# Gate scaling and two kinds of copies moved from VectorE to ScalarE in a fused transform, routing and expert kernel

## The chip, the cores and the metric

The kernel runs on one core of a Trainium2 chip. The metric is the device time of one execution in microseconds (us), lower is better. Engines are called as in the profile: PE is TensorE, DVE is VectorE, ACT is ScalarE, POOL is GpSimd, SP is SyncE, which only issues transfers. Each engine works through its own queue in order; a queue whose first instruction waits holds everything behind it.

## The reference

Three stages follow one another.

1. A spectral layer on x (4 x 3072 x 256): a real Fourier transform over the 3072 positions, a complex 256x256 product with bias, a soft threshold of 0.01, and the inverse transform. The result is read as 12288 rows of 256 numbers.
2. A routed expert layer with 8 experts and room for 384 rows in each. A row goes to the expert with its largest logit (row times a 256x8 matrix), if a place is left in order of the rows, and the output is scaled by the softmax weight of that expert, the gate:

```python
h = np.maximum(np.einsum('ecd,edf->ecf', disp, w1), 0.0)
y = np.einsum('ecf,efd->ecd', h, w2)
out[i] = gate_w[i] * y[expert_idx[i], pos[i]]
```

3. A dense layer: `h = x @ w_in` (256 to 2048), `g = h * sigmoid(h)`, `g @ w_out` (2048 to 256). Rows without a place are zero all through.

## The kernel before, in words

All matmuls that need it are made of three products of rounded parts: a number is split into a rounded part ("hi", cast by ACT at L192) and the remainder ("lo", a subtraction by DVE or POOL at L200), and `mm3` (L206) issues hi x hi, lo x hi and hi x lo. So each tile that PE reads has an ACT cast and a DVE or POOL subtraction ahead of it.

The first part of the kernel (`near`, to about 175 us) does the spectral layer of the first batch and the forward part of the second, and routes the first 3072 rows. The kernel then turns only as many rows of the second batch as it needs to fill the experts: `third` (L569) does the inverse transform of a third of that batch in four blocks of 512 columns. In it `rows` loads the spectrum that `kphase` stored (its last blocks are copied by ACT at L495 through `hi`, L192) and turns it by matmuls; ACT copies the result to SBUF (L595) and SP stores it. `gate` (L600) transposes the rows on PE, **copies the transposed rows from PSUM (L606)**, multiplies them by the gate matrix, and for every second block chooses the expert of each row on DVE (`choose`). `route` (L696) then gives each row its place, and `slots` (L804) makes the list of rows and gate weights `gw` for each expert.

`experts` (L949) runs the experts in the order 0, 1, 2, first pair, 3, 4, second pair, 5, 6, third pair, 7, fourth pair; `third` and `route` run beside experts 0 to 2. For each expert:

- `gather` (L1078) fetches its 384 rows by three indirect transfers that POOL issues.
- `turn` (L1092) **scales each of the three 128-row pieces by the gate weight of its rows (L1095)**, one number per partition, transposes the pieces on PE (L1102), and splits the result (ACT cast, DVE remainder). The gate weight is not negative, so it can be applied ahead of the layer. For all but the first expert the turn is issued in step 6 of the part before, and `behind` ties the scaling to a DVE instruction of step 5 there; the tie is an order for the planner and no semaphore.
- `first_ffn` (L1106) makes the hidden layer in 8 steps: PE fills a PSUM tile, ACT rectifies it (L1120), DVE makes the remainder (L1121), PE multiplies with the second weights. At its end **the two halves of the expert's output are copied from PSUM: the first by ACT (L1130), the second by DVE (L1131)**.
- `weights` (L1051) loads weight pieces through four buffers by SP (L1066), ACT casts them and DVE or POOL makes the remainders.

`pair` (L1133) takes the outputs of two experts, combines them by additions and subtractions on DVE (L1151 to L1159) and splits the combinations into `ms` tiles; `second_ffn` (L1166) runs the dense layer on both with seven products in place of eight per block, the gated unit by ACT (L1199), and writes the rows out by indirect transfers.

The order within each engine's queue isn't written out by hand: the program is traced in the order of the code, and a planner that simulates the engines' times settles the order of every queue when the kernel is built (`schedule_with_timeline_sim=True`, L1387). A change of an instruction's engine can so change the order of others too.

Of the kernel before, what the change touches and what calls it, by code (L numbers as in the profile page):

```python
# [12 lines left out]
ALU = mybir.AluOpType  # L13
AF = mybir.ActivationFunctionType
# [121 lines left out]
def raw(t):  # L136
    return t.bitcast(F32)
# [18 lines left out]
class Kernel:  # L156
# [412 lines left out]
    def third(self, b, res):  # L569

        nc, bp, ps, wg, CH = self.nc, self.bp, self.ps, self.wg, self.CH
        v = nc.vector
        c4 = self.c4[:Q, 64:]
        bv = self.bds[b].rearrange("k (r u g) c -> (k r) u (g c)", r=4, u=4)
        od = self.attn[0][b * S:b * S + QB * TW].rearrange("(q u g) d -> u q (g d)", u=4, g=GT)
        res[b] = self.chosen(1)
        idle = self.mg.tile([P, 3, 2, CH], F32, tag="ms", name="bi", bufs=1)
        room = {n + 2: idle[:Q, n] for n in range(3)}
        room[5] = self.mh.tile([P, 2, CH], F32, tag="yT", name="by", bufs=1)[:Q]

        def rows(n):
            pt = ps.tile([P, CH], F32, tag="ps", name="ps2")
            for w in range(2):
                br = room.get(2 * n + w)
                if br is None:
                    br = bp.tile([Q, 2, CH], F32, tag="xt", name="br", bufs=self.sb)
                nc.sync.dma_start(out=br, in_=bv[:, 2 * w:2 * w + 2, n * CH:(n + 1) * CH])
                for z in range(2):
                    u = 2 * w + z
                    ins = nc.tensor.matmul(pt[u * QB:(u + 1) * QB], c4, br[:, z], start=True, stop=True).ins  # L590
                    if b == 1 and not u:
                        self.after(ins, self.lasty)
            ao = bp.tile([P, 2, 2, P], F32, tag="ao", name="ao2")
            aof = ao.rearrange("p g h d -> p (g h d)")
            nc.scalar.copy(aof, pt)  # L595
            for u in range(4):
                nc.sync.dma_start(out=od[u, :, n * CH:(n + 1) * CH], in_=aof[u * QB:(u + 1) * QB])
            return ao

        def gate(n, ao):  # L600
            tp = ps.tile([P, 2, 2, P], F32, tag="ps", name="tp")
            for g in range(2):
                for h in range(2):
                    nc.tensor.transpose(tp[:, g, h], ao[:, g, h], self.ident)
            aT = bp.tile([P, 2, 2, P], F32, tag="aT", name="aT", bufs=1)
            v.tensor_copy(aT, tp)  # L606
            if n % 2 == 0:
                self.lg = ps.tile([P, P], F32, tag="ps", name="lg")
            for h in range(2):
                for g in range(2):  # L610
                    at = COL * (2 * (n % 2) + g)
                    nc.tensor.matmul(self.lg[at:at + COL], wg[:, h], aT[:, g, h], start=h == 0, stop=h == 1)
            if n % 2:
                ls = bp.tile([P, P], F32, tag="ls", name="ls", bufs=1)
                nc.scalar.copy(ls, self.lg)
                lt = ps.tile([P, 4, COL], F32, tag="ps", name="lt")
                nc.tensor.transpose(lt.rearrange("p g e -> p (g e)"), ls, self.ident)
                self.choose(lt.rearrange("p (o g) e -> p o g e", o=1)[:, :, :, :E], res[b], slice(2 * n - 2, 2 * n + 2))

        ao = {}  # L620
        for n in range(GT // 2 + 1):
            if n < GT // 2:
                ao[n] = rows(n)
            if n:
                gate(n - 1, ao.pop(n - 1))
            yield

    def is2(self, b, qbs, res):
# [58 lines left out]
        for g in range(GT + 2):  # L687
            if g < GT:
                ao[g] = rows(g)
            if 0 < g <= GT:  # L690
                aT[g - 1] = turn(ao.pop(g - 1))
            if g > 1:
                gate(g - 2, aT.pop(g - 2))
            yield
# [397 lines left out]
    def turn(self, rows, behind=None):  # L1092
        xg, gw = rows
        for j in range(SC):
            ins = self.nc.vector.tensor_scalar(xg[:, j], xg[:, j], gw[:, j:j + 1], None, ALU.mult)  # L1095
            if behind:
                self.after(ins.ins, behind)
        xT = self.mx.tile([P, 2, 2, CAP], FR, tag="xT", name="xT")
        for h in range(2):
            tp = self.ph.tile([P, CAP], F32, tag="hp", name="gtp")  # L1100
            for j in range(SC):
                self.nc.tensor.transpose(tp[:, j * P:(j + 1) * P], xg[:, j, h * P:(h + 1) * P], self.ident)  # L1102
            self.split("av", xT[:, 0, h], xT[:, 1, h], tp)
        return xT

    def first_ffn(self, e, xT, ws):  # L1106
        nc, mp, pm = self.nc, self.mh, self.pm
        NJ = F // P
        w1, w2 = ws
        yp = [pm.tile([P, 2 * D], F32, tag="y", name=f"y{h}")[:, :CAP] for h in range(2)]  # L1110
        hs = {}
        for j in range(NJ + 1):
            if j < NJ:
                hp = self.ph.tile([P, CAP], F32, tag="hp", name="hp")
                for h in range(2):
                    w, c = w1[j // 2], slice(j % 2 * P, (j % 2 + 1) * P)
                    self.mm3(hp, w[:, 0, h, c], w[:, 1, h, c], xT[:, 0, h], xT[:, 1, h], h == 0, h == 1)
                hh = mp.tile([P, CAP], FR, tag="hh", name="hh")
                hl = mp.tile([P, CAP], FR, tag="hl", name="hl")
                self.rectified = nc.scalar.activation(hh, hp, AF.Relu).ins  # L1120
                self.evicted = nc.vector.scalar_tensor_tensor(hl, hp, 0.0, raw(hh), ALU.max, ALU.subtract).ins  # L1121
                hs[j] = hh, hl
            if j > 0:
                hh, hl = hs.pop(j - 1)
                for h in range(2):
                    w, c = w2[(j - 1) // 2], slice(h * P, (h + 1) * P)
                    self.lasty = self.mm3(yp[h], w[:, 0, (j - 1) % 2, c], w[:, 1, (j - 1) % 2, c], hh, hl, j == 1, j == NJ)[1]
            yield
        y = self.ys[e] = self.mg.tile([P, 2, CAP], F32, tag="yf", name="yf", bufs=3)
        nc.scalar.copy(y[:, 0], yp[0])  # L1130
        nc.vector.tensor_copy(y[:, 1], yp[1])  # L1131

    def pair(self, behind=None):  # L1133

# [256 lines left out]
```

## Time and profile before

| what | us |
|---|---|
| median of 3 runs (lowest to highest) | 616.54 (615.39 to 617.16) |
| time of the profiled execution | 617.55 |
| its span, first to last instruction | 615.8 |
| PE busy in the span | 593.4 |
| DVE busy | 424.7 |
| ACT busy | 339.3 |
| POOL busy | 187.0 |

The profile is of one execution; its times are counted from its first instruction. "L1095" is line 1095 of the kernel. A matmul row gives the shape of the weights and the moving data; a row with "xN" merges N instructions that follow one another. Rows of neighbouring instructions on one engine overlap by about 0.09 us. What stands in brackets behind a row is the time that the engine stood still before it and what ended that. PEclk is the granted clock of TensorE as a share of its upper level (2.4 GHz; the lower, 1.2 GHz, is 0.50).

### The profile page before, as it was taken

Reading aid. Unit: us, or ns where it says so; the run is one execution under the profiler, and the core shown is the slowest. Engines: PE = TensorE matmul, PEld = TensorE weight load, DVE = VectorE, ACT = ScalarE, POOL = GpSimd, SP = SyncE. Lnnn points to the kernel's source line nnn. Section 1 sums busy time; section 2 is a strip of 40 time slices with the busy share of each in tenths; the row PEclk is TensorE's granted clock in tenths of the full one; section 3 lists DMA queues with packets and bytes.
Section 4 is the critical chain, followed back from the end, with each engine's and each line's share of the span. In section 5 each row is a group of like instructions: output and inputs, shape, how many; then the busy total and the mean of one; then the engine's idle time right before and its main releaser. Section 6 shows DMA issues by size and latency. Waiting matters only on the chain. (4 is left out here: it accounts for less than half of the span.)

```text
span 615.8 us, 11426 instructions
## 1 busy us (share of the span) xinstructions
PE 593.4 (96%) x4104; PEld 556.1 (90%) x4104; DVE 424.7 (69%) x844; ACT 339.3 (55%) x723; POOL 187.0 (30%) x189
## 2 busy tenths in 40 slices
PE   9999999999989799899999999999999999999994
PEld 9887799667988589789999999999999999989994
DVE  2468765449977589998876786587587577486563
ACT  2546554336525465556765756655567556365562
POOL 1001110002053023177453505435403442154433
PEclk9999999999999799989999999999999999999998
DMA  8829775996357976433633532404433230010001
GB/s 223 254 78 277 249 219 168 250 278 180 105 183 209 248 226 191 143 120 99 197 120 116 169 125 97 155 23 138 150 113 106 91 100 26 0 65 27 16 2 56
DMA packets 65755, 86.09 MB, mean 140 GB/s; under 512 B 5812, under 2 KB 55608, under 8 KB 65688
## 3 DMA queue, kind: packets, MB, share of 16 engines
q1 hardware_dynamic: 53720, 69.53, 37.8%
q10 hardware_dynamic: 9664, 9.44, 5.2%
q0 software_dynamic: 2304, 6.29, 3.2%
q8 instruction: 34, 0.56, 0.4%
q14 instruction: 33, 0.27, 0.2%
HBM read 54.31 MB, written 30.93 MB: 138 GB/s over the span
## 5 line engine op out<-in xcount | busy, mean ns | idle before, releaser
L1289 DVE TENSOR_TENSOR u<-h,u 128x384 f32<-128x384 f32 x224 | 117.9, 552 | 59.9 <-PE h L210 51.6
L1199 ACT ACTIVATE u<-u 128x384 f32<-128x384 f32 x128 | 64.6, 522 | 73.1 <-DVE u L1289 71.1
L209 PE MATMUL o<-wo,gl 128*128 128x256 f32 x354 | 94.5, 280 | 0.9 <-DVE gl L200 0.9
L210 PE MATMUL o<-wo,gh 128*128 128x256 f32 x354 | 94.6, 280 | 0.0
L208 PE MATMUL o<-wo,gh 128*128 128x256 f32 x354 | 83.1, 280 | 0.0
L200 POOL TENSOR_TENSOR ring<-mt,ring 128x384 fp32r<-128x384 f32 x32 | 38.0, 1190 | 136.3 <-ACT ring L192 136.3
L200 POOL TENSOR_TENSOR gl<-u,gh 128x384 fp32r<-128x384 f32 x62 | 64.8, 1060 | 29.6 <-ACT gh L192 29.5
L209 PEld LDWEIGHTS o<-wo,gl 128*128 128x128 f32 x354 | 66.5, 188 | 1.2 <-DVE gl L200 1.2
L210 PEld LDWEIGHTS o<-wo,gh 128*128 128x128 f32 x354 | 66.5, 188 | 0.0
L192 ACT CAST gh<-u 128x384 fp32r<-128x384 f32 x126 | 63.1, 509 | 5.7 <-PE o L210 4.0
L208 PEld LDWEIGHTS o<-wo,gh 128*128 128x128 f32 x354 | 62.4, 188 | 0.0
L208 PE MATMUL yp<-wri,xk 128*128 128x256 f32 x188 | 56.1, 298 | 0.0
L210 PE MATMUL yp<-wri,xk 128*128 128x256 f32 x188 | 54.0, 287 | 0.0
L209 PE MATMUL yp<-wri,xk 128*128 128x256 f32 x188 | 53.7, 286 | 0.0
L192 ACT CAST w<-st 128x512 fp32r<-128x512 f32 x64 | 38.6, 619 | 23.5 <-DMA st<-in_moe_w 15.7
L200 DVE TENSOR_TENSOR w<-st,w 128x512 fp32r<-128x512 f32 x56 | 39.6, 717 | 17.1 <-ACT w L192 12.0
L1120 ACT ACTIVATE hh<-hp 128x384 fp32r<-128x384 f32 x64 | 31.1, 489 | 35.4 <-PE y L209 13.7
L1121 DVE SCALAR_TENSOR_TENSOR hl<-hp,hh 128x384 fp32r<-128x384 f32 x64 | 34.9, 552 | 21.6 <-ACT hh L1120 16.3
L200 POOL TENSOR_TENSOR wi<-na,wi 128x256 fp32r<-128x256 f32 (+1 forms) x8 | 8.1, 1012 | 132.9 <-ACT wi L192 132.9
L208 PE MATMUL hp<-xT,w 128*128 128x384 f32 x128 | 43.8, 343 | 4.2 <-ACT w L192 4.1
L200 DVE TENSOR_TENSOR gl<-u,gh 128x384 fp32r<-128x384 f32 x64 | 42.8, 669 | 2.2 <-ACT gh L192 2.1
L208 PE MATMUL y<-hh,w 128*128 128x384 f32 x128 | 43.7, 341 | 0.5 <-ACT hh L1120 0.5
(254 smaller groups left out, 1543.1 us busy)
## 6 DMA issues: line engine op xcount, KB each, us to landing
st<-in_moe_w SPq DMA_DIRECT2D x64, 256.0 KB, 2.9
out<-zt SPq DMA_DIRECT2D x48, 256.0 KB, 3.5
b_d<-bo ACTq DMA_DIRECT2D x12, 512.0 KB, 3.1
mt<-mixed SPq DMA_DIRECT2D x32, 192.0 KB, 2.3
xt<-in_x SPq DMA_DIRECT2D x15, 384.0 KB, 6.7
nt<-in_moe_w_in SPq DMA_DIRECT2D x8, 512.0 KB
nt<-in_moe_w_out SPq DMA_DIRECT2D x16, 256.0 KB, 3.0
a_d<-ao SPq DMA_DIRECT2D x8, 384.0 KB, 3.4
```

The costliest lines, as they stand in the source:

```text
L192: self.lastact = self.nc.scalar.copy(dst, src)
L200: return e.tensor_tensor(dst, src, raw(hi), ALU.subtract).ins
L208: first = nc.tensor.matmul(out, lh, rh, start=start, stop=False)
L209: nc.tensor.matmul(out, ll, rh, start=False, stop=False)
L210: return first.ins, nc.tensor.matmul(out, lh, rl, start=False, stop=stop).ins
L1120: self.rectified = nc.scalar.activation(hh, hp, AF.Relu).ins
L1121: self.evicted = nc.vector.scalar_tensor_tensor(hl, hp, 0.0, raw(hh), ALU.max, ALU.subtract).ins
L1199: act.activation(sg, sg, AF.Silu)
L1289: v.tensor_tensor(to, h, u, ALU.add)
```

## The change

Three kinds of instructions go from DVE to ACT: the scaling of the gathered rows by their gate weight (24 instructions, 128x256 each, an ACT activation with function Copy and a scale of one number per partition), the copy of the transposed rows of the turned third (4 instructions, 128x512) and the copy of the second half of the expert outputs (8 instructions, 128x384). The data, the tiles and the transfers are the same.

```diff
@@ gate, in third
-            v.tensor_copy(aT, tp)
+            nc.scalar.copy(aT, tp)
@@ turn
-            ins = self.nc.vector.tensor_scalar(xg[:, j], xg[:, j], gw[:, j:j + 1], None, ALU.mult)
+            ins = self.nc.scalar.activation(xg[:, j], xg[:, j], AF.Copy, scale=gw[:, j:j + 1])
@@ first_ffn
         nc.scalar.copy(y[:, 0], yp[0])
-        nc.vector.tensor_copy(y[:, 1], yp[1])
+        nc.scalar.copy(y[:, 1], yp[1])
```

## Rows read from the trace of the kernel before

**Rows 1.** The page's busy times of the engines, share of the span, instructions.

```profile
PE 593.4 (96%) x4104; PEld 556.1 (90%) x4104; DVE 424.7 (69%) x844; ACT 339.3 (55%) x723; POOL 187.0 (30%) x189
```

**Rows 2.** Stretches: bounds, length, busy time of each engine, PEclk, DMA share, GB/s.

```profile
178.00:186.00 8.00, 6.11 (x42) 5.37 (x41) 5.75 (x12) 3.44 (x7) 6.21 (x6) 1.00 0.79 247
...
204.60:211.30 6.70, 6.69 (x24) 4.59 (x25) 3.00 (x5) 2.87 (x6) 0.00 (x0) 0.50 1.09 258
...
262.20:266.00 3.80, 3.80 (x13) 3.70 (x13) 3.05 (x10) 0.68 (x1) 3.49 (x3) 0.55 0.24 72
...
290.00:598.00 308.00, 306.89 (x2085) 305.31 (x2084) 213.53 (x395) 187.77 (x403) 118.44 (x111) 1.00 0.29 92
```

**Rows 3.** Groups that the change removes: busy us, mean ns, idle before.

```profile
L1095 DVE TENSOR_SCALAR xg<-xg,gwt 128x256 f32<-128x256 f32 x15 | 9.7, 699 | 0.0
...
L1131 DVE COPY yf<-y 128x384 f32<-128x384 f32 x8 | 4.4, 555 | 1.4 <-PE y L210 1.2
...
L1095 DVE TENSOR_SCALAR xg<-xg,gws 128x256 f32<-128x256 f32 x9 | 3.6, 438 | 2.2 <-DMA xg<-attn,srcs 2.2
...
L606 DVE COPY aT<-tp 128x512 f32<-128x512 f32 x4 | 2.7, 675 | 0.0
```

**Rows 4.** Groups of ACT nearest to what the change adds, same columns.

```profile
L462 ACT ACTIVATE xk<-xk 128x256 fp32r<-128x256 f32 x22 | 9.1, 416 | 0.0
...
L1130 ACT COPY yf<-y 128x384 f32<-128x384 f32 x8 | 3.8, 470 | 2.0 <-PE y L210 2.0
...
L753 ACT ACTIVATE pm<-iota,r 128x128 fp32r<-128x128 f32 x8 | 2.4, 389 | 0.6 <-DVE r L737 0.6
...
L595 ACT COPY ao<-ps 128x512 f32<-128x512 f32 x4 | 2.3, 585 | 1.9 <-PE ps L590 1.9
...
L462 ACT ACTIVATE xk<-xk 128x128 fp32r<-128x128 f32 x2 | 0.6, 298 | 0.0
```

**Rows 5.** In order of time, first turn: start, us, instruction, idle before.

```profile
178.26 1.32 ACT L192 CAST w<-st 128x512 fp32r<-128x512 f32 x2 [6.47 <-DMA st<-in_moe_w]
...
179.48 0.58 ACT L192 COPY bo<-bp 128x512 f32<-128x512 f32 x1
...
179.99 0.35 DVE L1095 TENSOR_SCALAR xg<-xg,gws 128x256 f32<-128x256 f32 x1 [2.17 <-DMA xg<-attn,srcs]
...
182.67 0.34 DVE L1095 TENSOR_SCALAR xg<-xg,gws 128x256 f32<-128x256 f32 x1
...
183.07 0.44 PE L1102 MATMUL gtp<-ident,xg 128*128 128x128 f32 x2 [0.93 <-DVE xg L1095]
...
183.84 0.58 ACT L192 COPY bo<-bp 128x512 f32<-128x512 f32 x1 [3.77 <-PE gtp L1102]
...
184.47 1.13 PE L494 MATMUL bp<-cl,c 128*128 128x256 f32 x4 [0.97 <-ACT bo L192]
```

**Rows 6.** In order of time, the first pair.

```profile
260.40 0.44 PE L208 MATMUL h<-ms,wi 128*128 128x384 f32 x1 [1.22 <-ACT ms L192]
260.53 0.55 DVE L1131 COPY yf<-y 128x384 f32<-128x384 f32 x1
...
262.17 0.45 PE L210 MATMUL h<-ms,wi 128*128 128x384 f32 x1 [1.15 <-DVE ms L200]
```

**Rows 7.** ACT and PE in order of time, second turn and weights.

```profile
203.94 0.62 ACT L192 CAST w<-st 128x512 fp32r<-128x512 f32 x1 [5.88 <-DMA st<-in_moe_w]
...
204.61 0.69 PE L208 MATMUL hp<-xT,w 128*128 128x384 f32 x1 [4.11 <-ACT w L192]
...
207.74 1.54 PE L1102 MATMUL gtp<-ident,xg 128*128 128x128 f32 x6
...
207.90 0.59 ACT L595 COPY ao<-ps 128x512 f32<-128x512 f32 x1 [1.95 <-PE ps L590]
```

**Rows 8.** ACT and DVE in order of time, the last copy of the third.

```profile
237.74 0.62 ACT L192 CAST wo<-na 128x512 fp32r<-128x512 f32 x1 [2.37 <-DVE na L900]
...
238.10 0.67 DVE L606 COPY aT<-tp 128x512 f32<-128x512 f32 x1
```

## The prediction

> **What bounds the kernel now.** I read the page's line of busy times first, then a table of stretches, then the order of time around every stretch in which PE stands still. The first shows PE busy in 593.4 us of a span of 615.8, DVE in 424.7 and ACT in 339.3 [rows 1]. The change touches only DVE and ACT, so it can be worth something only where PE waits for one of them. The table of stretches says where that is: from 290 to 598 us PE is busy for 306.9 of 308.0 us, so at most 1.1 us is to be had there [rows 2]. What the change can reach lies between 178 and 266 us, in three places.
>
> - The first turn (expert 0): PE waits 0.93 us for the third scaling of gathered rows and 0.97 us for a copy of ACT [rows 5].
> - The weights of the first experts: PE waits 4.11 us for a cast of ACT that itself waited for a weight load [rows 7], and then runs 6.7 us at a mean granted clock of 0.50, the lower of its two levels (1.2 GHz), which costs 6.7 x 0.50 = 3.4 us [rows 2].
> - The first pair: PE waits 1.22 us for a cast and 1.15 us for a remainder of the combined expert outputs [rows 6], and the clock then averages 0.55 for 3.8 us, which costs 3.8 x 0.45 = 1.7 us [rows 2].
>
> **Prices.** Removed from DVE: 24 scalings, 9.7 + 3.6 us; four copies of the turned third, 2.7 us; eight copies of half an expert output, 4.4 us: 20.4 us together [rows 3]. Added to ACT: a copy of the turned third has the form of the ACT copy at L595, 0.585 us; a copy of half an output that of L1130, 0.470 us, so 4 x 0.585 + 8 x 0.470 = 6.1 us [rows 4]. A scaling by ACT whose factor is one number per partition is not in the trace. Without such an operand, 128x256 takes 0.416 us and 128x128 takes 0.298 (L462); with one, 128x128 takes 0.389 (L753). The low end is therefore 0.416; the high end is 0.389 + (0.416 - 0.298) = 0.507. I take 0.50, near the high end, because the operand is there: 24 x 0.50 = 12.0 us. ACT comes to 339.3 + 18.1 = 357.4 us and DVE to 404.3; neither becomes the bound of the whole.
>
> The Trainium skill, in "ScalarE: Activation LUTs", section "What ACT_TABLE_LOAD costs", gives 186 ns plus 0.833 ns per element and about 93 ns more for each pointer operand. By that a scaling would be an estimated 0.49 us, and the 24 of them 11.8 us instead of 12.0.
>
> **The first turn.** In the trace ACT casts two weight pieces at 178.26, copies a spectrum block at 179.48 until 180.06, and then stands still until 183.84, when PE's transposes of the gathered rows end [rows 5]. DVE begins the first scaling at 179.99, as its gather lands, and the third at 182.67, with no wait for a transfer listed [rows 5]. So the third gather had landed before 182.67, by how much is not shown. If it was there by 181.6, ACT, idle from 180.06, ends the third scaling at 182.1, against 182.67 + 0.34 = 183.01 now; if it came only at 182.67, at 183.17. I take the first, since DVE shows no wait there: PE's wait of 0.93 shrinks by 0.9 us. The wait of 0.97 us moves along, because the copy that ends it is released by the same transposes. The best case loses both waits, 1.9 us. The worst is a price of the in-order queue: if the planner sets the scalings ahead of the two casts and the copy at 178.26 to 180.06, those 1.8 us follow the last scaling, and PE's matmuls behind that copy come up to 1.7 us later. No DMA is moved; the gathers stay on POOL and the weight loads on SP.
>
> **The second and third turn, the weights.** The 4.11 us wait ends with a weight load, and the DMA share is 1.09 in the stretch after it [rows 2, 7]. Three scalings off DVE do not move that: zero. The tie of the scalings to a DVE instruction of the step before ("behind") now names another engine; it is an order for the planner and no semaphore. What could be lost here is the second rival.
>
> **The first pair.** DVE's copy of half an output stands at 260.53 in front of the remainders on which PE waits until 262.17 [rows 6]. Without it those come 0.47 us earlier (0.555 less the overlap of neighbours of some 0.09). On ACT the added copy follows the one of the first half and delays the casts behind it by about 0.4 us, so the first wait grows from 1.22 to some 1.6 us while the second ends at 261.7: a gain of 0.5 us, between 0 and the whole 2.4. The clock is the larger term. PE's waits here, 2.37 us, were followed by the lower level; the 1.90 us of the first turn were not (1.00 over 178 to 186 us) [rows 2, 5, 6]. With 1.9 us left I count half of the 1.7 us, 0.9, and keep both ends.
>
> **Five later turns and the other copies: zero.** Their cover is the full queue of PE. The scalings of these turns average 0.699 us, where the one at 182.67 took 0.34, twice as long, and PE has no more than 1.1 us of idle time in the whole stretch [rows 2, 3, 5]. If the cover were thinner on ACT, where the step's rectified outputs queue behind three scalings of 1.3 us together, a turn would lose part of that; I keep +2 us for the five as the end.
>
> **Sum.** 0.9 + 0.5 + 0.9 = 2.3 us. The profiled execution took 617.55 us (span 615.8 and 1.75 around it), 1.0 above the median of the runs, 616.54; against itself it goes to 615.25, and the median goes to 614.2.
>
> **Rivals.**
>
> *The route is relieved too (chance 0.14).* The last copy of the turned third starts at 238.10 on DVE, while ACT stands still for 2.37 us until 237.74 [rows 8]. If the planner lets ACT do it there, the logits, the choice and the route come up to 2.3 us earlier, DVE reaches the pair that much sooner, and all of 2.37 + 1.7 = 4.1 us goes. With 0.9 of the first turn: 616.54 - 5.0 = 611.5. Against it: the planner fixes PE's order, and PE may take the logits no earlier.
>
> *Nothing moves (0.27).* The third gather lands late, the casts of the pair are pushed back by the copy that was put on ACT, the clock falls as before: 616.5. For it speaks that each gain stands behind a chain of several engines.
>
> *Slower, through ACT's queue in the second turn (0.23).* DVE scaled the rows of expert 1 at 200 us, while ACT stood 5.88 us at the weight cast of 203.94 [rows 7]. On ACT the scalings can come only before that cast or after it. If they come after the copy of the third that starts at 207.90 and ends at 208.49, they end at 209.8, and PE's transposes, now at 207.74, slip by 2.1 us; the engine is then at the lower level and stays there about as much longer, which costs half of that, 1.0 more. That is +3.1, and with nothing gained elsewhere 619.6. It decides from the point where the first of these scalings starts later than 207.74 - 1.3 = 206.4. Against it: before the cast ACT is free from 198.06 to 203.94, and the rows have long landed.
>
> A rule of the Trainium skill speaks for this side: "ScalarE: Activation LUTs", "Rules for kernel authors", tells authors to use VectorE, not ScalarE, for a multiplication or an addition. The rows agree as to one instruction, 0.34 us on DVE at 182.67 [rows 5] against my 0.50; by the rule alone the change would give away time on each turn, while the mean of 0.699 on DVE in the later turns goes against it.
>
> **How the numbers follow.** My forecast has 0.36, its own range 612.5 to 615.5. About 0.3% of the time, 1.85 us, is what a measurement of this kernel can tell from no change: below 614.7 is faster, above 618.4 slower. Of the forecast 0.31 lies below 614.7 and 0.05 above; with the relieved route's 0.14, faster is 0.45. The same: 0.05 + 0.27 + 0.01 = 0.33. Slower: 0.22 of the 0.23. The range runs from the relieved route, 611.3, to just short of the worst of the slower case, 619.3.
>
> **What would show it.** Right: the third scaling ends by 182.2 on ACT and PE's wait for it is below 0.2 us; ACT's scalings take 0.49 to 0.51; PE's wait at 262 us is near 0.7 and the half-clock stretch behind it shorter or gone; the 4.1 us wait for weights stays; from 290 us on PE's idle time stays near 1.1. Wrong: another order of the weight loads on SP, which would change the 4.1 us either way; a PE wait on the gathered rows in the second or third turn; new waits of PE for rectified outputs behind the scalings of later turns.

## The result: 0.8% slower, and the profile after

The changed kernel takes 621.36 us, median of 20 runs (618.58 to 626.12), against 616.56 for the kernel before in the same session (20 runs): ratio 1.0079, 95% interval 1.0060 to 1.0097. The forecast was 614.2 with a range up to 619.3; direction and range were both wrong. The profiled execution took 624.49 us, its span is 622.7.

The page's line of busy times answers to [rows 1]:

```profile
PE 592.7 (95%) x4104; PEld 553.0 (89%) x4104; DVE 408.0 (66%) x808; ACT 353.0 (57%) x759; POOL 182.9 (29%) x189
```

DVE lost 16.7 us, ACT gained 13.7, and PE does the same 4104 matmuls in the same time; the span is 6.9 us longer. So PE stands still more. The stretches, with the columns of [rows 2], say where:

```profile
178.00:186.00 8.00, 6.51 (x41) 5.39 (x41) 5.16 (x9) 4.70 (x10) 5.58 (x5) 1.00 0.78 249
...
262.20:266.00 3.80, 3.41 (x18) 2.77 (x17) 3.66 (x10) 2.40 (x6) 1.46 (x2) 1.00 0.00 0
290.00:342.00 52.00, 52.00 (x365) 52.00 (x364) 37.07 (x65) 34.68 (x77) 21.01 (x21) 1.00 0.42 130
342.00:374.00 32.00, 27.48 (x159) 26.48 (x158) 19.35 (x36) 18.38 (x40) 9.19 (x9) 1.00 0.44 135
374.00:598.00 224.00, 223.54 (x1531) 221.79 (x1530) 140.19 (x267) 139.14 (x302) 85.98 (x81) 1.00 0.25 78
290.00:598.00 308.00, 303.02 (x2051) 300.27 (x2050) 196.61 (x367) 192.20 (x416) 116.18 (x111) 1.00 0.30 93
```

In the kernel before, the fourth of these stretches reads:

```profile
342.00:374.00 32.00, 32.00 (x193) 31.63 (x192) 27.00 (x51) 22.34 (x49) 9.67 (x10) 1.00 0.46 145
```

All idle time that PE gained after 290 us lies between 342 and 374 us, 4.5 us of it, where expert 3 ends and expert 4 begins. I call that place the crossing. In the list of PE's waits over the whole execution (who waited, for whom: us in total, times, longest us), the second line, for the copy of half an output, is the longest single wait and lies at the crossing; of the first line 1.2 us do, and the other three lie before 290 us:

```profile
PE y L210 <- DVE hl L1121: 4.0, 4, 1.9
PE y L208 <- ACT yf L1130: 3.3, 1, 3.3
PE hp L208 <- ACT w L192: 2.6, 1, 2.6
PE y L208 <- ACT hh L1120: 1.9, 2, 1.5
PE lg L612 <- ACT aT L606: 1.4, 1, 1.4
```

The groups that were added to ACT (columns as in [rows 3]):

```profile
L1095 ACT ACTIVATE xg<-xg,gwt 128x256 f32<-128x256 f32 x15 | 6.5, 499 | 0.0
...
L1095 ACT ACTIVATE xg<-xg,gws 128x256 f32<-128x256 f32 x9 | 4.1, 503 | 1.7 <-DVE cl L487 1.3 <-DMA xg<-attn,srcs 0.4
L1131 ACT COPY yf<-y 128x384 f32<-128x384 f32 x8 | 3.9, 488 | 0.0
...
L606 ACT COPY aT<-tp 128x512 f32<-128x512 f32 x4 | 2.3, 581 | 0.0
```

The prices were right: 0.499 and 0.503 us for a scaling (0.50 forecast), 0.488 and 0.581 for the copies (0.470 and 0.585). (ACT's total came to 353.0 and not to 357.4, DVE's to 408.0 and not to 404.3: the forecast added up single prices, and neighbouring rows overlap by some 0.09 us, which makes about 3 us of either difference.) The estimate by the Trainium skill ("ScalarE: Activation LUTs", "What ACT_TABLE_LOAD costs"), 0.49 for a scaling, agrees with the trace too. The time was not lost on prices.

### The profile page after: what moved, and what is told of

It is laid out like the page before. It is cut to its first block, busy times and chain, and to the rows that moved or that the text cites. A ratio compares the mean times of both kernels' runs of the same rounds, so it can differ in the third digit from the quotient of the medians.

```text
span 622.7 us, 11433 instructions
## 1 busy us (share of the span) xinstructions
PE 592.7 (95%) x4104; PEld 553.0 (89%) x4104; DVE 408.0 (66%) x808; ACT 353.0 (57%) x759; POOL 182.9 (29%) x189
## 5 line engine op out<-in xcount | busy, mean ns | idle before, releaser
L200 POOL TENSOR_TENSOR ring<-mt,ring 128x384 fp32r<-128x384 f32 x32 | 36.6, 1144 | 134.6 <-ACT ring L192 131.9
L200 POOL TENSOR_TENSOR gl<-u,gh 128x384 fp32r<-128x384 f32 x62 | 63.5, 1041 | 39.1 <-ACT gh L192 37.8
```

The costliest lines, as they stand in the source:

```text
L200: return e.tensor_tensor(dst, src, raw(hi), ALU.subtract).ins
```

## The experiments

Each was timed beside the kernel before on the same chip; the ratio is to that. "Crossing" below is also a time: from PE's first transpose of expert 4's rows to the first L1230 of the second pair, the product that opens its output rows: 24.9 us before, 30.0 after. In edits that add lines, the line numbers of the rows are up to 8 higher.

### One part at a time

In the four expectations of this group theory A blames the scalings, theory B the copies of half an output, and theory C the copies of the turned third. Behind them the letters are given anew.

**Only the scalings on ACT** (the hunk of `turn` alone):

> Only the 24 scalings go to ACT; the copy of the turned third and the half outputs stay on DVE. Theory A (the scalings, set three in a row into ACT's queue ahead of the copies of finished output rows and of the rectified step outputs, are what PE pays for): 3 to 6 us slower than before, with a new wait of PE of over 1 us where expert 3 ends. Theory B (the half-output copies, queued on ACT behind a rectified output that waits, hold the PSUM tile of the next expert): 0 to 1 us from before, no such wait. Theory C (the relief of the turned third moves the order around 240 to 255 us): within 1 us of before, with the 2.4 us of PE waits at the first pair as before.

Measured: 622.01 us, ratio 1.0101 [1.0076, 1.0126]. PE waits 2.0 us at the crossing, runs 3.4 us at the lower clock behind it, and the crossing takes 28.9 us: what A expected.

**Only the copies of half an output** (the hunk of `first_ffn` alone):

> Only the eight half-output copies go to ACT. Theory A: within 1 us of before. Theory B: 3 to 6 us slower, with PE waiting over 1 us on the copy at L1130 or L1131 where expert 3 ends. Theory C: within 1 us of before; at the first pair the second wait of PE about 0.5 us shorter.

Measured: 616.91 us, ratio 1.0011 [0.9998, 1.0024]; PE waits 0.2 us at the crossing.

**Only the copies of the turned third** (the hunk of `gate` alone):

> Only the four copies of the turned third go to ACT. Theories A and B: within 1 us of before, from 290 us on unchanged. Theory C: the wait of PE moves from the first pair (2.4 us at 260 us) to remainders of the last expert step before it (1.9 us at 251 us in the changed kernel), and the time is 1 to 2 us above before.

Measured: 614.29 us, ratio 0.9962 [0.9942, 0.9983]: faster, where theory C had expected one to two microseconds more.

**The whole change once more**, in the same session:

> The changed kernel once more, for a second trace: 621.4 us, 4.8 above before. Theory A and B: the 3.3 us wait of PE near 352 us, on the first half copy of expert 3's output, is there again, within 1 us. If it is under 1 us here, the stall of that one execution is chance and cannot carry the median's 4.8 us.

Measured: 620.18 us, ratio 1.0069 [1.0049, 1.0090]; crossing 30.5 us, and PE's wait is there again, 2.8 us long. The parts, +5.6, +0.5 and -2.1 us by medians against 616.39, add up to +4.0, the whole is +3.8. The scalings are what costs.

### What happens at the crossing

ACT's queue there, in the changed kernel:

```profile
340.75 1.31 ACT L1095 ACTIVATE xg<-xg,gwt 128x256 f32<-128x256 f32 x3
341.97 1.05 ACT L1240 COPY tail<-o 128x512 f32<-128x512 f32 x2
...
348.62 0.49 ACT L1120 ACTIVATE hh<-hp 128x384 fp32r<-128x384 f32 x1 [1.09 <-PE hp L210]
352.23 0.62 ACT L192 CAST w<-st 128x512 fp32r<-128x512 f32 x1 [3.12 <-PE hp L210]
354.38 0.49 ACT L1120 ACTIVATE hh<-hp 128x384 fp32r<-128x384 f32 x1 [1.53 <-remote]
354.77 0.47 ACT L1130 COPY yf<-y 128x384 f32<-128x384 f32 x1
```

and two of PE's instructions:

```profile
348.58 0.33 PE L210 MATMUL hp<-xT,w 128*128 128x384 f32 x1
...
355.29 0.44 PE L208 MATMUL y<-hh,w 128*128 128x384 f32 x1 [3.26 <-ACT yf L1130]
```

Read them together. The three scalings are over at 342.06; they are not in the way of anything at 350. The weight cast of 352.23 waits for the matmul that began at 348.58 and took 0.33 us, the last reader of its buffer: it starts 3.3 us after that matmul's end. The copy behind it in ACT's queue comes at 354.77, and PE waits 3.26 us for the PSUM tile that this copy empties. The weight load had landed by 345 us. So for some microseconds PE's finished work is not seen by the engines that wait for it. The trace holds the semaphore events of PE, by which it tells the others that a matmul is done; set against the ends of matmuls (which the profile models), 585 of 628 come within 0.02 us, but here they are up to 3.89 us late.

What else ran there is on POOL. Before, the indirect transfers that write the first pair's rows out (L1337, two for each third of the rows, called scatters below) and the gathers of expert 6 (L1084) are spread from 333 us:

```profile
333.15 1.02 POOL L1337 DMA_INDIRECT out<-tail,dsts  x1 [3.79 <-ACT tail L1240]
334.48 1.00 POOL L1337 DMA_INDIRECT out<-tail,dsts  x1 [0.30 <-issue]
339.52 1.34 POOL L1337 DMA_INDIRECT out<-tail,dsts  x1 [4.04 <-ACT tail L1240]
341.17 0.98 POOL L1337 DMA_INDIRECT out<-tail,dsts  x1 [0.30 <-issue]
342.46 1.44 POOL L1337 DMA_INDIRECT out<-tail,dsts  x1 [0.30 <-issue]
...
348.15 1.00 POOL L1084 DMA_INDIRECT xg<-attn,srct  x1 [0.30 <-issue]
```

After, nine of them follow one another every 1.3 us:

```profile
342.81 1.02 POOL L1337 DMA_INDIRECT out<-tail,dsts  x1 [10.39 <-ACT tail L1240]
344.14 1.00 POOL L1337 DMA_INDIRECT out<-tail,dsts  x1 [0.30 <-issue]
...
353.28 1.16 POOL L1084 DMA_INDIRECT xg<-attn,srct  x1 [0.30 <-issue]
```

What releases the scatters of a row third is ACT's copy of it (L1240). Before, the three copies came at 332.3, 338.7 and 340.6:

```profile
332.29 0.58 ACT L1240 COPY tail<-o 128x512 f32<-128x512 f32 x1 [0.33 <-PE o L210]
338.66 0.59 ACT L1240 COPY tail<-o 128x512 f32<-128x512 f32 x1 [0.34 <-PE o L210]
340.64 0.59 ACT L1240 COPY tail<-o 128x512 f32<-128x512 f32 x1 [0.68 <-issue]
```

With the scalings on ACT the planner sets the copies of the first two row thirds behind them, and all three start between 342.0 and 343.3 us. It also set PE's own order anew: the products that close the first two thirds end at 340.9 and 341.2 there, so that without the scalings these copies could have come about 1 us earlier and no more.

```profile
340.64 0.28 PE L210 MATMUL o<-wo,gh 128*128 128x256 f32 x1
...
340.88 0.40 PE L210 MATMUL o<-wo,gh 128*128 128x256 f32 x2
```

That gave theory A: the unbroken run of indirect transfers makes PE's completions late. Theory B: the scalings hold ACT's queue.

**The bunch without the scalings.** The kernel before, its copies of output rows held back; every queue but ACT's is the same, instruction for instruction.

```diff
                 if m == 5:
                     behind = self.evicted
+                    if ph == 3:
+                        self.sixth = self.rectified
...
-            act.copy(oo, self.op[s_])
+            copy = act.copy(oo, self.op[s_]).ins
+            if q == 1:
+                self.after(copy, self.sixth)
```

> The kernel before, all scalings and copies as they were; only the first pair's three copies of output rows (L1240) are put behind ScalarE's rectified block 6 of expert 3, so that they come in a bunch, as they do in the changed kernel. Theory A (the six scatters of the first pair and the three gathers of expert 6 then run back to back on POOL, nine indirect transfers from about 339 to 351 us instead of two, then seven, and while so many run PE's completions reach the other engines late; the late casts and copies cost PE a wait and a stretch at half clock where expert 3 ends): 2 to 6 us slower than before, 618.5 to 622.5, with completions of PE over 1 us late near 350 us, although ScalarE has not one scaling more. Theory B (the three scalings themselves hold ScalarE's queue, 1.3 us at the crossing): within 0.3% of before, no PE wait there.

Measured: 618.86 us, ratio 1.0038 [1.0012, 1.0065]. With no scaling on ACT the same wait is there, in the list of waits and in the stretch behind it (clock 0.57):

```profile
PE y L208 <- ACT yf L1132: 2.8, 1, 2.8
```

```profile
348.00:356.00 8.00, 6.16 (x20) 6.16 (x21) 7.70 (x16) 5.52 (x13) 0.00 (x0) 0.57 0.40 117
```

Its crossing takes 30.5 us. Theory B cannot make this; A's range holds it. The profiled execution took 620.57 us, where the ten go from 615.47 to 620.76, so its 5.6 us at the crossing stand beside a median of only 2.4 us more.

**The gathers taken away from the run**, first with the scalings alone, then in the whole change:

```diff
@@ gather
+            if s == 6:
+                self.after(ins.ins, self.pooled)
@@ the second pair's remainders on POOL
+            elif q == 1 and j < 2:
+                self.pooled = low
```

> The fifteen scalings on ScalarE; only the gathers of expert 6 are put behind POOL's first residues of the second pair, some 20 us later than with the scalings alone, so that the six scatters run without three gathers at their heels. ScalarE's queue is the same, word for word. Theory A: completions of PE late by 0.3 to 1.6 us at most at the crossing as other runs of six show, PE's wait of 2.0 us there gone with the half clock behind it, 617 to 619 us (the early loss of some 2 us stays). Theory B (ScalarE's queue): as with the scalings alone, 621 to 623 us.

Measured: 619.21 us, ratio 1.0046 [1.0028, 1.0063], 2.8 us less than with the scalings alone; crossing 27.3 us. Half of the loss came back; the time is just above the upper end of what A expected and below B's range. PE's own order differs from that of the scalings alone in 13 of 4104 places. The lower clock at the crossing is gone, but PE still stands still 2.1 us there, which A had not expected.

> The changed kernel with expert 6's gathers put behind POOL's first residues of the second pair. Theory A: the 3 to 5 us that the crossing from expert 3 to 4 costs come back, 615 to 618 us. Theory B: 620 to 621.5 us, as the changed kernel.

Measured: 619.26 us, ratio 1.0049 [1.0025, 1.0074]; crossing 27.0. A miss for A's numbers, and below B's too: six scatters in a row are still enough to cost 2 us there.

**Expert 4's scalings back on DVE**, the others on ACT:

> The scalings on ScalarE but for the three of expert 4, which stay on VectorE; ScalarE has no scaling within 20 us of the crossing from expert 3 to 4, but the order of the first pair's row copies (two in a row behind expert 3's weight casts) is still that of the scalings' kernel. Theory A (the bunched scatters and gathers): still slow there, 620 to 623 us, PE waits over 1 us at the crossing and its completions come over 1 us late. Theory B (1.3 us of scalings in ScalarE's queue): the wait at the crossing is gone, 617 to 619 us.

Measured: 618.32 us, ratio 1.0029 [1.0007, 1.0052]; no wait of PE, crossing 25.2. Against A as it was put, and what B expected. In the trace the nine transfers are there, but with three breaks (starts at 339.6, 341.5, 342.8, 344.3, ... 349.5, 351.2), so no more than five are unbroken. The 0.3% that remain were not lost at the crossing; where is not shown.

**Only POOL's order changed**, the first two scatters set behind the next two:

```diff
+                ins = out(q - 1, s_, oo, e)
+                if q == 1 and s_ < 2 and not self.again:
+                    self.two[s_].append(ins)
+            if q == 1 and s_ == 1 and not self.again:
+                for ins in self.two[0]:
+                    self.after(ins, self.two[1][-1])
```

> The kernel before with the queues of all other engines the same, instruction for instruction: only on POOL the two scatters of the first row third (at 333.2 and 334.5 us before) are put behind the two of the second, so that six scatters and three gathers run one after the other from 339.5 us. Theory A (a long unbroken run of indirect transfers makes PE's completions late for the other engines): completions over 1 us late near 350 us, PE waits there, 2 to 5 us slower than before, 618.5 to 621.5. Theory B (what cost time in the bunched kernel was the order of ScalarE's queue): within 0.3% of before, no PE wait there.

Measured: 616.17 us, ratio 1.0000 [0.9983, 1.0017]. A's number missed again, and B's was met; looked at afterwards, the trace shows the same as the one before: the nine ran from 337.1 to 349.7 with three breaks, five at most unbroken. Their number is not what counts.

What opens a break can be read from the traces. POOL's pause between two that are ready is the same 0.30 us; at a break one of them takes 1.25 to 1.6 us itself, and it is one that starts while DVE makes a weight remainder, or within 0.03 us of that. In the kernel before, for the scatters at 339.52 and 342.46:

```profile
339.32 0.68 DVE L200 TENSOR_TENSOR w<-st,w 128x512 fp32r<-128x512 f32 x1
...
342.35 0.69 DVE L200 TENSOR_TENSOR w<-st,w 128x512 fp32r<-128x512 f32 x1 [1.79 <-issue]
```

Over all 14 traces, from 200 us on, 42 indirect transfers start under a weight remainder, and 40 of them end 0.84 to 0.91 us after its end; of the 504 others, 500 take 1.2 us or less. So whether a run of nine breaks hangs on where DVE's remainders fall. In the changed kernel only two of the nine start under one: the third, just as it ends, and the last. No run tried this by itself.

**The run broken up.** Two fills of a scratch tile on POOL behind each of the six scatters, by which the gathers come ahead of the last four of them (the expectation says five); the queues of the other engines are the same, instruction for instruction.

```diff
+                ins = out(q - 1, s_, oo, e)
+                if q == 1 and not self.again:
+                    if self.gap:
+                        self.after(ins, self.gap)
+                    for _ in range(2):
+                        fill = nc.gpsimd.memset(self.filler, 0.0).ins
+                        self.after(fill, ins)
+                    self.gap = fill
```

> The fifteen scalings on ScalarE, every queue but POOL's the same, instruction for instruction; on POOL two fills of a scratch tile stand behind each of the six scatters of the first pair, and expert 6's gathers come ahead of the last five scatters, so that no more than four indirect transfers follow one another unbroken. Theory A: completions at the crossing late by 0.7 us at most, PE's wait of 2.0 us and the half clock behind it gone, 617 to 619 us. Theory B (ScalarE's queue): 621 to 623 us, as with the scalings alone.

Measured: 616.96 us, ratio 1.0016 [0.9998, 1.0034]; crossing 24.9 us, as before, and PE without a wait in it. POOL's order of time there:

```profile
340.64 1.02 POOL L1345 DMA_INDIRECT out<-tail,dsts  x1 [10.40 <-ACT tail L1241]
341.67 0.69 POOL L1248 MEMSET filler<- 128x256 f32 x2
342.82 1.32 POOL L1345 DMA_INDIRECT out<-tail,dsts  x1 [0.45 <-issue]
...
351.00 2.94 POOL L1345 DMA_INDIRECT out<-tail,dsts  x1 [0.46 <-issue]
```

and the copy that PE had waited for:

```profile
347.85 0.47 ACT L1131 COPY yf<-y 128x384 f32<-128x384 f32 x1
```

The same edit in the whole change:

> The whole change, every queue but POOL's the same, instruction for instruction; on POOL two fills of a scratch tile stand behind each of the first pair's six scatters and expert 6's gathers come ahead of the last five, so that no long unbroken run of indirect transfers is left at the crossing from expert 3 to 4. Theory A (that run is what the change lost by): PE's wait there is gone, the stretch from expert 4's transposes to the second pair's first L1230 back to 24.9 us (before; 30.0 in the changed kernel), 614.5 to 617 us. Theory B (ScalarE's longer queue, or the early stretches, hold most of the loss): 618.5 to 621 us.

Measured: 614.88 us against 615.81 before, ratio 0.9991 [0.9979, 1.0003]; crossing 25.3 us. The ratio of the scalings alone fell by 0.0085, that of the whole change by 0.0078 against its second timing, with no instruction moved on any engine but POOL. Both are as A expected (the first 0.04 us below its range), and B is out. Two stretches of the whole change, broken up:

```profile
342.00:374.00 32.00, 31.77 (x197) 31.11 (x196) 23.94 (x46) 21.70 (x47) 17.48 (x21) 1.00 0.51 157
...
290.00:598.00 308.00, 306.01 (x2075) 303.91 (x2074) 201.28 (x374) 194.41 (x421) 121.01 (x121) 1.00 0.29 92
```

The table sets the profiles side by side. Worked out from instruction and semaphore records: "unbroken" is the longest run of indirect transfers whose starts are at most 1.45 us apart, "late" the latest completion of PE against the end of its matmul, "idle" PE's idle time, all at the crossing, in us. All but the ratio is of one profiled execution.

```
kernel                    unbroken  late  idle  crossing  ratio to before
before                       4      0.32  0.0    24.9     1
third alone                  4      0.02  0.0    24.9     0.9962
half alone                   4      0.23  0.2    25.3     1.0011
POOL's order                 5      1.10  0.0    24.8     1.0000
expert 4's on DVE            5      1.22  0.0    25.2     1.0029
bunch, no scalings           5      2.04  2.8    30.5     1.0038
change, gathers later        6      1.49  1.6    27.0     1.0049
scalings, gathers later      6      1.53  2.1    27.3     1.0046
scalings alone               9      3.72  2.1    28.9     1.0101
change, second time          9      3.77  2.8    30.5     1.0069
change                       9      3.89  4.5    30.0     1.0079
scalings, broken up          3      0.02  0.0    24.9     1.0016
change, broken up            3      0.02  0.2    25.3     0.9991
third and half               4      0.02  0.2    25.3     0.9984
```

Up to 1.2 us of lateness cost PE nothing, from 1.5 us on it waits. The length of the run alone does not set the lateness (2.04 and 1.22 us with five). The lower clock follows some of these waits and not others: 6.8 us of it in the bunch and in the change's second profile, 3.4 behind the scalings alone, none behind the change's own 4.5 us. That is part of why equal runs cost unequal time.

**The change without its scalings:**

> The change without its scalings: the turned third and the second half output copied by ScalarE, the scalings on VectorE. If the parts add up (third alone 2.1 us faster, half alone 0.5 slower), 614.0 to 615.5 us; no wait of PE over 1 us at the crossing from expert 3 to 4. Rival (the two crowd ScalarE together): 616 to 618 us.

Measured: 615.10 us, ratio 0.9984 [0.9966, 1.0003]. The parts add up. The third alone has the lowest ratio of all, 0.9962, faster than both kernels.

## Why the prediction was wrong

**"Five later turns and the other copies: zero" is the step that failed**, and "Their cover is the full queue of PE" the reason that did not hold. PE had 1.1 us of idle time in that stretch [rows 2], and I took a full queue for a safe one. One of the five turns, expert 4's, cost 5.1 us in the profile (30.0 - 24.9), beyond the +2 kept for all five. The mechanism named for that end, rectified outputs queued behind 1.3 us of scalings, is not what cost it. What the runs showed in its place is nine indirect transfers in an unbroken run, under which PE's completions came up to 3.9 us late. "No DMA is moved", written for the first turn, looked at who issues a transfer and not at what releases it: the scatters stand on POOL as before, but ACT's copies of rows release them, and the planner moved those, and PE's products ahead of them, together. No rival had this. That the run then met no break was luck, as far as the traces tell: it hung on where DVE's remainders fell.

The mean of 0.699 us in that step is a misreading too. The fifteen scalings it stands for took either 0.34 us (eight, expert 4's among them) or 1.10 us (seven, each while POOL made a remainder); none took 0.7. For expert 4 the move was from 0.34 to 0.50 us.

**The slower rival** had the right sign and the wrong place. In the second turn the scalings run ahead of the weight cast, as the argument against it said:

```profile
198.02 1.29 ACT L1095 ACTIVATE xg<-xg,gws 128x256 f32<-128x256 f32 x3
204.21 0.62 ACT L192 CAST w<-st 128x512 fp32r<-128x512 f32 x1 [4.89 <-DMA st<-in_moe_w]
```

The rule quoted beside it, from the Trainium skill ("ScalarE: Activation LUTs", "Rules for kernel authors"), speaks against this change and the time agrees with it, but the price of the instruction is not the reason: with the run broken up, the same scalings on ACT cost 0.16% [-0.02%, 0.34%], which is not clear of zero.

**The second and third turn** were put at zero. PE's wait of 4.1 us for the weight cast is 2.6 us in the changed kernel, and 0.9 and 1.8 in two other profiles with its queues; with the queues of before it is 4.1, 2.5 and 3.1. The weight loads ahead of it stand in the same order. The lower clock behind it lasted 6.8 us in the profile before and 3.4 us in the two others with its queues. Both differ that much from one execution to the next, so the sign that the wait stays can neither be called met nor missed.

**The first turn** chose the wrong end. The third gather came late, and ACT waited for it until 182.58:

```profile
182.58 0.51 ACT L1095 ACTIVATE xg<-xg,gws 128x256 f32<-128x256 f32 x1 [0.39 <-DMA xg<-attn,srcs]
```

The third scaling starts 2.3 us after the first (2.5 and 2.25 us in two other profiles with these queues), where the prediction needed 1.6, and ends at 183.09 instead of 182.1. PE's wait for it is gone, but the planner set a cast and a copy of ACT behind the first scaling, a part of the worst case named, and PE waits 0.55 us behind the copy: from 178 to 186 us PE stands still 1.49 us, against 1.89, so 0.4 of the 0.9 us came.

**The first pair.** The copy of half an output, taken from DVE, was to give 0.5 us; alone it gives nothing (1.0011). In its profile PE's two waits of 2.37 us have become one of 0.8, but PE stands still 2.43 us from 258 to 272 us, against 2.59 before: the waiting moved. The half clock at 262 us is gone in the changed kernel (clock 1.00 in the second stretch above), but from 251.4 to 254.8 us the clock is at that level, behind a wait of PE of 1.9 us for a remainder. Nor was it steady before: of three profiles with the queues of before up to there, one (the bunch's) has no lower clock at the pair.

**The route rival** (0.14) has its sign in the third alone, which gained 2.1 us of the 4.1 that this rival gives to the route. In its profile the logits start 3.05 us after the last transposes of the third, against 4.1 to 4.6 in three profiles with the queues of before, so PE did take them earlier; and PE's two waits at the pair are 0.80 and 0.54 us, against some 1.2 and 1.15 in those three. PE has no idle time between 240 and 258 us, where the kernel before has 0.53, and the clock does not fall behind that (0.88 before, but 1.00 in the bunch's profile too):

```profile
240.00:258.00 18.00, 18.00 (x110) 17.97 (x109) 16.60 (x51) 10.53 (x21) 4.85 (x5) 1.00 0.66 220
258.00:272.00 14.00, 10.66 (x56) 8.51 (x55) 13.76 (x29) 7.36 (x17) 8.77 (x8) 1.00 0.42 131
```

What of this makes the gain was not tried: the first L1230 comes at 266.0 us, and at 268.4, 264.4 and 265.8 in those three.

**The sum.** With the run broken up the change comes to 0.9991 of before, some 0.6 us faster and not clear of zero [0.9979, 1.0003]; the forecast of 2.3 us less was too high even without the crossing, by the first turn and the pair. (The lower end of the range, 611.3, is not the route rival's sum, 611.5; nothing hangs on it.)

## What to carry to other kernels

An engine that is full in every slice is no cover: ask what each moved instruction stands ahead of in its new queue, and which transfers those instructions release. When a wait's releaser ended long before the wait did, look for what else ran at that time, and take that apart with every other queue held the same. A change in several parts should be timed part by part: here one part gained 0.4%, and another took 1%. Before a single profile is believed, take a second one of the same queues.

## What was not expected of the hardware

While indirect transfers follow one another without a break on POOL, the completions of PE's matmuls reach ACT and DVE late: at the crossing by 0.32 us at most with three or four in a row, 1.1 to 2.0 us with five, 1.5 with six, 3.7 to 3.9 with nine. DVE's and ACT's own completions there are never more than 0.02 us late in the changed kernel. Where the length is the same it is not constant: the six scatters near 545 us in the kernel before made 0.53 us. By what path the one holds up the other no run here shows.

DVE's weight remainders lengthen an indirect transfer on POOL that starts under them, to 0.84 to 0.91 us behind their end in 40 of 42 cases. The scatter of 2.94 us in the run with fills (0.98 in a plain run) fits that and not the fills: from its start at 351.00 DVE works without a pause on tiles in SBUF, a weight remainder among them, until 353.07, and the scatter ends 0.87 us later. That it is these instructions of DVE and nothing beside them was not tried.

One kernel's early part differs from one execution to the next: the first pair's L1230 came at 269.3, 267.1 and 263.0 us in three profiles of the change that have the same queues up to there (the last with the run broken up later). A single profile's times before 290 us do not tell two kernels apart; the medians do.
